# A linear-attention and SwiGLU block in split fp32: the gate and up operands' low parts from a PSUM copy, stores of h sums by SyncE a step later, eight weight-sum jobs beside the attention product

## The chip, the cores and the metric

The kernel runs on one core of a Trainium2 chip. The metric is the device time of one execution in microseconds (us); the median of three runs is given, with a profiled execution beside them whose trace the text reads. Five engines matter: TensorE (PE, matrix products; PEld loads its weights), VectorE (DVE), ScalarE (ACT), GpSimd (POOL) and SyncE (SP, which only issues DMAs here). Each works through its own queue in order.

## The reference

S = 2048 tokens, D = 1024, F = 3584, 32 heads of 32, all in fp32.

```python
def _A_ref(x, wqkv, wo):
    qkv = (x @ wqkv).reshape(B, S, 3, H, Dh)   # q, k, v by head
    phi = lambda t: where(t > 0, t + 1, exp(t)) + 1e-6
    pq, pk = phi(q), phi(k)
    kv = einsum("bhsd,bhse->bhde", pk, v)
    z = einsum("bhsd->bhd", pk)
    num = einsum("bhqd,bhde->bhqe", pq, kv)
    den = einsum("bhqd,bhd->bhq", pq, z)[..., None] + 1e-6
    return (num / den).reshape(B, S, D) @ wo

def _B_ref(x, w1, w3, w2):
    h = silu(x @ w1) * (x @ w3)
    return h @ w2

xn = layernorm(x)
s = _A_ref(xn, A_wqkv, A_wo)
out = x + s * silu(_B_ref(xn, B_w1, B_w3, B_w2))
```

## The kernel before

**Products.** Every fp32 operand is split into a high part, a cast to fp32r on ACT (L103), and a low part, the difference of operand and high part on DVE (L104). A matmul of fp32 is three of fp32r, hi·hi, hi·lo, lo·hi, at L109, L110 and L111. A matrix product is cut into 2x2 blocks and made of seven block products instead of eight (`gemm`), so operands are sums of blocks: A, S, S1 and so on of the tokens, B11, B12, T1 to T4 of the weights, the latter made by DVE (`combine`, L471) in the tile of raw weights and then split by `ready` (L463). The seven products of a gemm run into PSUM banks named a to e with the gemm's name; DVE adds them up (L601 to L640; L579 copies one on ACT). `gu0_3` stands for u (combined sum) of gate gemm 3 in half 0.

**Stages.** The tokens come in two halves, h = 0 and 1. `half(h)` runs the key gemms (k), the query gemms (q), then 14 pairs of a gate gemm (g) and an up gemm (u). In half 1 the keys' rows are also turned on PE, kept in tiles y00, y01, y10, r2 and stored to y_d for the attention's sums. After the second half comes the attention product in eight steps m of `Segment.tokens` (`around(m)` hooks work into them), then the output stage: 26 block products of h with w2, whose operands are sums of blocks of h (h_d) and of w2 (wt_d).

**Sums on GpSimd.** After each gate and up pair the blocks of h are added up for the output stage (`later_sums`, `early_sums`, from L940, operations at L916 and L919) and stored to h_d from POOL's queue: `store_rows` (L925), `store_both` (L929). The sums of w2 are 28 jobs (`WSUMS`, seven t by four parts), each with a load by SP, eleven GpSimd operations (L1041 to L1055, written at L1021 to L1059) and three stores by SP to wt_d (L1039). Sixteen of them (`NOW`) come in half 0, appended to `next_work` behind the preparation of half 1's tokens; twelve in half 1 (`last_weight_sums`).

**What sets the order.** `catch_up` is called between block products. It moves the first generator of h sums (`hsums`) on by a step, then either a late piece (`later`) or a step of the first job (`jobs`). What is left at the end of a half is run there. The order inside each engine comes from a scheduler that lists the program by a simulated time; tiles and PSUM banks are given out then. Tiles come from pools: eight PSUM banks (tag of `bank`), four "job" tiles shared by the weight sums, the last h sums, y01 and y10 (`job_tile`) and the first operand loads of the attention product (r0q, r2q, ...), six small "c" tiles (among them the s tiles), ten operand tiles (`operand`).

The weight sums' steps:

```python
e.tensor_sub(out=o1[:, 0:2], in0=some(r, 0, 6), in1=some(r, 1, 6))
...
store(0, o1)
yield True
...
store(8, o2)
...
store(16, r[:, 0:2])
yield True
```

Of the kernel before, what the change touches and what calls it, by code (L numbers as in the profile page):

```python
# [16 lines left out]
P = 128  # L17
# [5 lines left out]
def tile_linear_attention_times_swiglu(  # L23
# [27 lines left out]
    def bank(name):  # L51
        return ps.tile([P, C], F32, tag="bank", name=name)
# [44 lines left out]
    def split(pair, src, negated=False):  # L97

        hi, lo = pair if isinstance(pair, tuple) else (pair[:, 0], pair[:, 1])
        if negated:  # L100
            nc.scalar.mul(hi, src, -1.0)
            return nc.vector.scalar_tensor_tensor(lo, src, -1.0, hi.bitcast(F32), op0=ALU.mult, op1=ALU.subtract)
        nc.scalar.copy(out=hi, in_=src)  # L103
        return nc.vector.tensor_sub(out=lo, in0=src, in1=hi.bitcast(F32))  # L104
# [32 lines left out]
    def job_tile(shape, name):  # L137
        return praw.tile(shape, F32, tag="job", bufs=4, name=name)
# [284 lines left out]
    class Operands:  # L423
# [37 lines left out]
            return self.B[n], self.b[n]  # L461

        def ready(self, n):  # L463
            split(*self.place(n))

        def combine(self, n, sums={"T1": ("B12", "B11", "B11"), "T2": ("B22", "T1", "T1"),
                                   "T3": ("B22", "B12", "B12"), "T4": ("B21", "T2", "T2")}):
# [74 lines left out]

    def catch_up(*marks):

        if hsums and next(hsums[0], done) is done:
            hsums.pop(0)
        for e in later:
            e[0] -= 1
        if later and later[0][0] <= 0:
            with ExitStack() as behind:  # L550
                for m in marks[-1:]:
                    behind.enter_context(tc.issue_after(m.ins))
                later.pop(0)[1]()
        elif jobs:
            job, in_order = jobs[0]
            with ExitStack() as behind:
                for m in marks + (tuple(fetched) if in_order else ()):
                    behind.enter_context(tc.issue_after(m.ins))
                if next(job, None) is None:
                    jobs.pop(0)  # L560
# [239 lines left out]
    def half(h):  # L800
        A = operand_tiles(h)

        def keys(pair, **how):
            return gemm(ops[f"k{h}_{pair}_"], A, uses[pair], **how)

        def run(g):
            for _ in g:
                pass

        def side_by_side(*gemms):  # L810
            for _ in zip_longest(*gemms):
# [12 lines left out]
        uses = [key_rows(h, pair) for pair in range(ND // 2)]  # L824
        if h == 0:
            early = [ops[f"k0_{pair}_"] for pair in range(ND // 2)]
            m = [keys(pair, early=True, own=pair == 0, led=pair == 0) for pair in range(ND // 2)]
            some = mybir.EngineType
            with tc.manual_schedule(engines={some.PE, some.Activation, some.DVE, some.Pool}):
                last = Opening(A, early, m).run()  # L830
            for k in early[2:]:
                k.ask()
            early[2].then = early[3].next
        else:

            ops["q1_0_"].ask()
            for i, n in enumerate(AOPS):
                with ExitStack() as behind:
                    if i > 1:
                        behind.enter_context(tc.issue_after(ops["q1_0_"].asked.ins))  # L840
                    for k in range(ND // 2):
                        nc.sync.dma_start(out=A[n][:, :, k].bitcast(F32), in_=a_d[n][:, :, k])
        if h == 0:
            with tc.issue_after(last.ins):
                for g in m:
                    run(g)
        else:
            side_by_side(keys(0, paired=True), queries(0, paired=True))
            for pair in range(1, ND // 2):
                run(keys(pair))  # L850
                run(queries(pair))
            jobs.append((all_denominators(), False))
            for _ in row_products():
                pass
        jobs.append((attention_work(), False) if h else (next_work(), True))
        if h:
            jobs.append((last_weight_sums(), False))
        if h == 0:
            for pair in range(ND // 2):
                run(queries(pair))  # L860
        for pair in range(NF // 2):
            last = h < NH - 1 and pair == NF // 2 - 1
            gemms = [gemm(ops[f"{'gu'[e]}{h}_{pair}_"], A, use, paired=last) for e, use in enumerate(hidden(h, pair))]
            if last:
                side_by_side(*gemms)
            else:
                for g in gemms:
                    run(g)
        for j, _ in jobs:
            run(j)  # L870
        jobs.clear()
        if h:
            for j in hsums:
                run(j)
            hsums.clear()

    def four_sums(x1, x2, s12, s34, e=nc.gpsimd):

# [42 lines left out]
    def quarter(tiles):  # L921
        return {f"{m}{'abcd'[k]}": a[:, :, m * P:(m + 1) * P] for k, a in tiles.items() for m in range(QT)}

    def store_rows(h, t, p, src):
        nc.gpsimd.dma_start(out=h_d[h][:, HROWS.index(p), :, t], in_=src)  # L925

    def store_both(h, t, p, src):
        i = HROWS.index(p)
        nc.gpsimd.dma_start(out=h_d[h][:, i:i + 2, :, t], in_=src)  # L929

    def sums_tile(name, place=None):
        a = (place or pc).tile([P, 2, 2, P], F32, tag="job" if place else "c", name=name, **({"bufs": 4} if place else {}))
# [85 lines left out]
        e.tensor_sub(out=b22, in0=b22, in1=b11)  # L1018
        e.tensor_sub(out=b21, in0=b21, in1=b22)

    def weight_sums(t, part, e=nc.gpsimd):  # L1021

        cols = slice(part * P, (part + 1) * P)

        def load():
            r = job_tile([P, 8, P], f"w2_{t}_{part}")
            rows = w2[4 * t * P:4 * (t + 1) * P, :].rearrange("(k p) (n c) -> p k n c", p=P, c=C)[:, :, :, cols]
            for i in range(4):
                nc.sync.dma_start(out=r[:, 2 * i:2 * i + 2], in_=rows[:, i])
            return r  # L1030

        def steps(r):
            o1, o2 = (job_tile([P, 8, P], f"w2s{t}_{part}_{i}") for i in range(2))

            def some(x, i, step):
                return x[:, i:i + step + 1:step]

            def store(i, x):
                nc.sync.dma_start(out=wt_d[t][:, i:i + x.shape[1], cols], in_=x)  # L1039

            e.tensor_sub(out=o1[:, 0:2], in0=some(r, 0, 6), in1=some(r, 1, 6))  # L1041
            e.tensor_add(out=o1[:, 2:4], in0=some(r, 0, 5), in1=some(r, 2, 5))
            e.tensor_add(out=o1[:, 4:6], in0=r[:, 2:4], in1=o1[:, 0:2])
            e.tensor_sub(out=o1[:, 6:8], in0=r[:, 4:6], in1=o1[:, 0:2])
            store(0, o1)
            yield True
            e.tensor_sub(out=o2[:, 0:2], in0=some(r, 0, 3), in1=some(r, 4, 3))
            e.tensor_sub(out=o2[:, 2], in0=o1[:, 2], in1=o1[:, 3])
            e.tensor_sub(out=o2[:, 3], in0=o1[:, 2], in1=r[:, 6])
            e.tensor_sub(out=o2[:, 4:6], in0=some(r, 2, 3), in1=o1[:, 5:7])  # L1050
            yield True
            e.tensor_sub(out=o2[:, 6:8], in0=some(o1, 4, 3), in1=r[:, 3:5])
            store(8, o2)
            e.tensor_add(out=r[:, 0], in0=r[:, 1], in1=o2[:, 1])
            e.tensor_add(out=r[:, 1], in0=o2[:, 0], in1=o2[:, 1])  # L1055
            store(16, r[:, 0:2])
            yield True

        return Job(load, steps)  # L1059

    WSUMS = [(t, part) for t in range(NQ) for part in range(4)]
    NOW = 16

    def next_work():

        yield from go_on([prepare_next(i) for i in range(TH // 2)])
        yield from go_on([weight_sums(*w) for w in WSUMS[:NOW]])

    def last_weight_sums():
        yield from go_on([weight_sums(*w) for w in WSUMS[NOW:]])  # L1070

    hm4 = const.tile([P, P // DH], F32, name="hm4")
    nc.vector.memset(hm4, 0.0)
# [447 lines left out]
    def left_early_split(s):  # L1521
# [2 lines left out]
            last = split((t[:, 0, k], t[:, 1, k]), a)  # L1524
        return last

    def around(m):
        if 2 <= m < NG - 1:
            for t in range(NQ):
                if t * 5 // NQ == m - 2:  # L1530
                    right_split(0, t, right_raw(0, t, small))
        if m == NG - 2:
            left_early(0, small)
            left_early_split(0)
# [103 lines left out]
```

## Time and profile before

| | us |
|---|---|
| median of three runs (2483.97 to 2487.59) | 2484.34 |
| the profiled execution | 2484.81 |
| its span in the trace | 2483.0 |
| PE busy | 2280.4 (92%) |
| DVE busy | 1714.3 (69%) |
| ACT busy | 926.3 (37%) |
| POOL busy | 914.0 (37%) |

Busy time is the time in which an engine works on instructions. A line of a timeline gives start, duration, engine, line of the kernel, operation, output<-inputs, shapes, and in brackets the idle time of the engine ahead of it with what ended it. SPq and POOLq rows are issues of DMAs. In a group of the page the last field is the idle time of the engine ahead of its instructions and its releaser. The granted clock is TensorE's, as a share of full speed.

### The profile page before, as it was taken

Reading aid. Unit: us, or ns where it says so; the run is one execution under the profiler, and the core shown is the slowest. Engines: PE = TensorE matmul, PEld = TensorE weight load, DVE = VectorE, ACT = ScalarE, POOL = GpSimd, SP = SyncE. Lnnn points to the kernel's source line nnn. Section 1 sums busy time; section 2 is a strip of 40 time slices with the busy share of each in tenths; the row PEclk is TensorE's granted clock in tenths of the full one; section 3 lists DMA queues with packets and bytes.
Section 4 is the critical chain, followed back from the end, with each engine's and each line's share of the span. In section 5 each row is a group of like instructions: output and inputs, shape, how many; then the busy total and the mean of one; then the engine's idle time right before and its main releaser. Section 6 shows DMA issues by size and latency. Waiting matters only on the chain. (4 is left out here: it accounts for less than half of the span.)

```text
span 2483.0 us, 30861 instructions
## 1 busy us (share of the span) xinstructions
PE 2280.4 (92%) x10584; PEld 1856.8 (75%) x10584; DVE 1714.3 (69%) x2534; ACT 926.3 (37%) x1554; POOL 914.0 (37%) x1211
## 2 busy tenths in 40 slices
PE   6999999998999999999999999994069999999999
PEld 5888777886777887778787778773057788888887
DVE  6988878868887775667857888887034455556576
ACT  5554333322222554433333332323022264444452
POOL 2221425489996411003445555566730100001010
PEclk8999999999999999999999999997589999999999
DMA  7555445566659637775646566657645485568596
GB/s 262 177 189 171 145 151 176 168 191 201 187 175 312 220 118 236 260 261 170 193 159 211 165 188 190 200 166 243 178 159 168 141 311 189 187 203 254 195 292 211
DMA packets 376062, 494.90 MB, mean 199 GB/s; under 512 B 23536, under 2 KB 264432, under 8 KB 375792
## 3 DMA queue, kind: packets, MB, share of 16 engines
q1 hardware_dynamic: 337952, 372.83, 47.0%
q0 software_dynamic: 37952, 120.09, 15.1%
q8 instruction: 83, 1.36, 0.2%
q14 instruction: 75, 0.61, 0.1%
HBM read 315.62 MB, written 180.88 MB: 200 GB/s over the span
## 5 line engine op out<-in xcount | busy, mean ns | idle before, releaser
L109 PE MATMUL o<-w,l 128*128 128x512 f32 x728 | 283.3, 389 | 0.0
L111 PE MATMUL o<-w,l 128*128 128x512 f32 x728 | 283.3, 389 | 0.0
L110 PE MATMUL o<-w,l 128*128 128x512 f32 x728 | 283.3, 389 | 0.0
L103 ACT CAST l<-lr 128x896 fp32r<-128x896 f32 (+1 forms) x106 | 98.6, 932 | 202.6 <-PE o L111 106.2
L104 DVE TENSOR_TENSOR l<-lr,l 128x896 fp32r<-128x896 f32 (+1 forms) x106 | 113.4, 1072 | 82.3 <-ACT l L103 81.6
L1432 POOL DMA_DIRECT2D out<-acc x14 | 12.0, 857 | 398.3 <-DVE acc L1430 393.1
L109 PEld LDWEIGHTS o<-w,l 128*128 128x128 f32 x728 | 136.7, 188 | 28.5
L110 PEld LDWEIGHTS o<-w,l 128*128 128x128 f32 x728 | 136.7, 188 | 28.3
L111 PEld LDWEIGHTS o<-w,l 128*128 128x128 f32 x728 | 136.7, 188 | 28.3
L104 DVE TENSOR_TENSOR xy<-xy,xy 128x512 fp32r<-128x512 f32 x112 | 72.6, 685 | 59.4 <-ACT xy L103 59.2
L1612 DVE TENSOR_TENSOR acc<-o,acc 128x512 f32<-128x512 f32 x64 | 43.7, 688 | 88.9 <-PE o L111 88.9
L109 PE MATMUL B11s<-wp,XA11s 128*128 128x512 f32 x4 | 2.2, 549 | 112.0 <-ACT XA11s L103 112.0
L103 ACT CAST xy<-xy 128x512 fp32r<-128x512 f32 x112 | 64.6, 620 | 85.8 <-PE g L111 45.8
L925 POOL DMA_DIRECT2D h_d<-h x70 | 50.5, 722 | 112.8 <-DVE h L907 71.5
L110 PE MATMUL g<-xy,xy 128*128 128x512 f32 x224 | 87.7, 392 | 0.3 <-DVE xy L104 0.3
L111 PE MATMUL g<-xy,xy 128*128 128x512 f32 x224 | 87.3, 390 | 0.0
L929 POOL DMA_DIRECT2D h_d<-hs x112 | 85.7, 766 | 4.1 <-POOL hs L919 3.0
L109 PEld LDWEIGHTS B11s<-wp,XA11s 128*128 128x128 f32 x4 | 1.1, 264 | 112.6 <-ACT XA11s L103 112.4
L109 PE MATMUL g<-xy,xy 128*128 128x512 f32 x224 | 81.0, 397 | 0.0
L664 POOL DMA_DIRECT2D y_d<-y x48 | 35.2, 742 | 124.1 <-ACT y L688 69.8
L1409 POOL DMA_DIRECT2D s_d<-s x32 | 17.3, 542 | 144.3 <-DVE s L1325 73.5
L104 DVE TENSOR_TENSOR w<-wr,w 128x512 fp32r<-128x512 f32 x98 | 63.0, 684 | 1.9 <-ACT w L103 1.8
(5247 smaller groups left out, 7295.5 us busy)
## 6 DMA issues: line engine op xcount, KB each, us to landing
lr<-h_d SPq DMA_DIRECT2D x102, 448.0 KB
wr<-wt_d SPq DMA_DIRECT2D x126, 256.0 KB
h_d<-hs POOLq DMA_DIRECT2D x112, 256.0 KB, 3.9
wt_d<-w2s SPq DMA_DIRECT2D x56, 512.0 KB
w<-in_B_w SPq DMA_DIRECT2D x112, 128.0 KB
xy<-x_d SPq DMA_DIRECT2D x28, 512.0 KB
xy<-y_d SPq DMA_DIRECT2D x28, 512.0 KB
wr<-in_B_w SPq DMA_DIRECT2D x56, 256.0 KB
```

What stands on the lines that cost most here:

```text
L103: nc.scalar.copy(out=hi, in_=src)
L104: return nc.vector.tensor_sub(out=lo, in0=src, in1=hi.bitcast(F32))
L109: nc.tensor.matmul(acc, lhsT=wh, rhs=ah, start=start, stop=False, skip_group_check=True)
L110: nc.tensor.matmul(acc, lhsT=wh, rhs=al, start=False, stop=False, skip_group_check=True)
L111: return nc.tensor.matmul(acc, lhsT=wl, rhs=ah, start=False, stop=stop, skip_group_check=True)
L664: nc.gpsimd.dma_start(out=y_d[h][:, :, YS.index(n), pair], in_=t.rearrange("p (t d) -> p t d", d=P))
L925: nc.gpsimd.dma_start(out=h_d[h][:, HROWS.index(p), :, t], in_=src)
L929: nc.gpsimd.dma_start(out=h_d[h][:, i:i + 2, :, t], in_=src)
L1409: nc.gpsimd.dma_start(out=s_d[2 * m + t][:, n * C:(n + 1) * C], in_=a)
L1432: nc.gpsimd.dma_start(out=out[rows, cols], in_=a, accum_op=ALU.add)
L1612: nc.vector.tensor_add(out=a, in0=b, in1=a)
```

## The change

Four edits.

1. `ready`: for gemms whose names begin with g or u, ACT casts the high part, then copies the operand into a PSUM bank of its own (named s, operand, gemm), and DVE subtracts the high part from that copy. The other gemms keep `split`.
2. `store_rows` and `store_both` put h sums' stores on a list, `store_all` issues them from SP at the next `catch_up`.
3. Twenty weight-sum jobs come in half 0, in a generator of their own marked "sums", behind the preparation; a step of it is made only where no h sums were pending. At the end of a half jobs are run until none is left.
4. The other eight jobs (t = 5, 6) run in the attention product, two in each of the steps 1 to 4, in the tiles of the first output step's weights (w0_1 to w0_6). The splits of these weights move from steps 2 to 6 to steps 4 to 7.

```diff
         def ready(self, n):
-            split(*self.place(n))
+            dst, src = self.place(n)
+            if self.name[0] in "gu":
+                nc.scalar.copy(out=dst[:, 0], in_=src)
+                copy = bank(f"s{n}{self.name}").rearrange("p (k s) -> p k s", s=P)
+                nc.scalar.copy(out=copy, in_=src)
+                nc.vector.tensor_sub(out=dst[:, 1], in0=copy, in1=dst[:, 0].bitcast(F32))
+            else:
+                split(dst, src)
...
     def catch_up(*marks):
+        busy = bool(hsums)
+        store_all()
         if hsums and next(hsums[0], done) is done:
             hsums.pop(0)
...
-        elif jobs:
+        elif jobs and not (busy and jobs[0][1] == "sums"):
...
         jobs.append((attention_work(), False) if h else (next_work(), True))
-        if h:
-            jobs.append((last_weight_sums(), False))
...
-        for j, _ in jobs:
-            run(j)
-        jobs.clear()
+        while jobs:
+            run(jobs.pop(0)[0])
         if h:
             for j in hsums:
-                run(j)
+                for _ in j:
+                    store_all()
             hsums.clear()
+            store_all()
...
     def store_both(h, t, p, src):
         i = HROWS.index(p)
-        nc.gpsimd.dma_start(out=h_d[h][:, i:i + 2, :, t], in_=src)
+        stores.append((h_d[h][:, i:i + 2, :, t], src))
+
+    def store_all():
+        for dst, src in stores:
+            nc.sync.dma_start(out=dst, in_=src)
+        stores.clear()
...
-    NOW = 16
+    NOW = 20
...
         yield from go_on([prepare_next(i) for i in range(TH // 2)])
-        yield from go_on([weight_sums(*w) for w in WSUMS[:NOW]])
-
-    def last_weight_sums():
-        yield from go_on([weight_sums(*w) for w in WSUMS[NOW:]])
+        jobs.append((go_on([weight_sums(*w) for w in WSUMS[:NOW]]), "sums"))
...
+    left_over = WSUMS[NOW:]
+
     def around(m):
-        if 2 <= m < NG - 1:
-            for t in range(NQ):
-                if t * 5 // NQ == m - 2:
-                    right_split(0, t, right_raw(0, t, small))
+        if 1 <= m < 5:
+            for e in range(2):
+                tags = iter([f"w0_{3 * e + i}" for i in range(1, 4)])
+
+                def place(shape, name):
+                    return pw0.tile(shape, F32, tag=next(tags), name=name)
+
+                job = weight_sums(*left_over.pop(0), place)
+                for _ in job.steps(job.load()):
+                    pass
+        for t in {4: [0], 5: [1, 2], 6: [3, 4], 7: [5, 6]}.get(m, []):
+            right_split(0, t, right_raw(0, t, small))
```

Three places in the order of the two programs. First POOL at the start of half 1, before: the last sums of half 0 (hs0_6, with their stores), then the stores of half 1's keys (pk, to pq_d) and of the turned rows (y00, y10, y01, to y_d1).

```order
L919 TENSOR_TENSOR hs0_6_16_6788<-h0_13_1_6422 128x256
L919 TENSOR_TENSOR hs0_6_16_6788<-hs0_6_16_6788,hk0_6_6317 128x256
L925 DMA h_d0_87<-hs0_6_16_6788 128x2x128
L820 DMA pq_d0_2_81<-pk1_0_0_6804 128x512
L664 DMA y_d1_134<-y00_1_0_6867 512x1x128
L664 DMA y_d1_134<-y10_1_0_6962 512x1x128
L820 DMA pq_d0_2_81<-pk1_1_0_6905 128x512
```

The changed program on POOL, ahead of the stores of the same y01 and y10: the end of the weight sums' job 4_2 and job 4_3 (w2s4_3_0 and _1 are its two tiles of sums).

```order
L1068 TENSOR_TENSOR w2s4_2_1_7000<-w2s4_2_0_6999,w2_4_2_6973 128x256
L1071 TENSOR_TENSOR w2_4_2_6973<-w2s4_2_1_7000 128x128
L1057 TENSOR_TENSOR w2s4_3_0_7015<-w2_4_3_6994 128x256
...
L1070 TENSOR_TENSOR w2_4_3_6994<-w2_4_3_6994,w2s4_3_1_7016 128x128
L673 DMA y_d1_134<-y01_1_0_7295 512x1x128
L1071 TENSOR_TENSOR w2_4_3_6994<-w2s4_3_1_7016 128x128
L673 DMA y_d1_134<-y10_1_0_7438 512x1x128 x2
```

Eight jobs, 3_0 to 4_3, now stand between the h sums of half 0 and these stores; before, none did.

ACT in half 0, before: the casts of up gemm 3's operands, with work of the preparation (L149) and of h (L903) between them.

```order
L103 CAST T3u0_3__2909<-wu0_3__2735 128x512
L149 ACT_TABLE_LOAD
L149 ACTIVATE y_2945<-v_2944 128x2
L103 CAST T2u0_3__2935<-wu0_3__2735 128x512
L103 CAST T1u0_3__2968<-wu0_3__2735 128x512
```

The same place in the changed program:

```order
L466 CAST T3u0_3__3009<-wu0_3__2818 128x512
L468 COPY sT3u0_3__3011<-wu0_3__2818 128x512
L466 CAST T2u0_3__3034<-wu0_3__2818 128x512
L468 COPY sT2u0_3__3036<-wu0_3__2818 128x512
L468 COPY sT1u0_3__3073<-wu0_3__2818 128x512
L468 COPY sB21u0_3__3099<-wu0_3__2818 128x512
L466 CAST T1u0_3__3071<-wu0_3__2818 128x512
L468 COPY sT4u0_3__3123<-wu0_3__2818 128x512
L468 COPY sB22u0_3__3147<-wu0_3__2818 128x512
```

Each operand has a copy to PSUM beside its cast, and several copies stand ahead of the casts of their operands.

POOL in the attention product, before: after the last store of h sums only the stores of s (s0_00 is step 0's block).

```order
L925 DMA h_d1_88<-hs1_6_16_14465 128x2x128
L1409 DMA s_d0_115<-s0_00_14622 128x512
L1409 DMA s_d1_116<-s0_11_14625 128x512
L1409 DMA s_d1_116<-s0_10_14624 128x512
L1409 DMA s_d0_115<-s0_01_14623 128x512
```

After:

```order
L1071 TENSOR_TENSOR w2_5_1_15399<-w2s5_1_1_15405 128x128
L1422 DMA s_d1_116<-s0_11_15241 128x512
L1422 DMA s_d1_116<-s0_10_15240 128x512
L1422 DMA s_d0_115<-s0_01_15239 128x512
L1057 TENSOR_TENSOR w2s5_2_0_15561<-w2_5_2_15556 128x256
L1058 TENSOR_TENSOR w2s5_2_0_15561<-w2_5_2_15556 128x256
L1063 TENSOR_TENSOR w2s5_2_1_15562<-w2_5_2_15556 128x256
L1422 DMA s_d3_118<-s1_11_15423 128x512
```

The stores of s stand between the weight sums' operations there.

More of the change, by code (lines that the diff above doesn't have):

```diff
@@ L922, in quarter @@
         return {f"{m}{'abcd'[k]}": a[:, :, m * P:(m + 1) * P] for k, a in tiles.items() for m in range(QT)}
+    stores = []
     def store_rows(h, t, p, src):
-        nc.gpsimd.dma_start(out=h_d[h][:, HROWS.index(p), :, t], in_=src)
+        i = HROWS.index(p)
+        stores.append((h_d[h][:, i, :, t], src))
     def store_both(h, t, p, src):
         i = HROWS.index(p)
-        nc.gpsimd.dma_start(out=h_d[h][:, i:i + 2, :, t], in_=src)
+        stores.append((h_d[h][:, i:i + 2, :, t], src))
[3 more added lines that the diff above has]
+        stores.clear()
     def sums_tile(name, place=None):
@@ L1019, in sums_of, with weight_sums @@
         e.tensor_sub(out=b21, in0=b21, in1=b22)
-    def weight_sums(t, part, e=nc.gpsimd):
+    def weight_sums(t, part, place=job_tile, e=nc.gpsimd):
         cols = slice(part * P, (part + 1) * P)
         def load():
-            r = job_tile([P, 8, P], f"w2_{t}_{part}")
+            r = place([P, 8, P], f"w2_{t}_{part}")
             rows = w2[4 * t * P:4 * (t + 1) * P, :].rearrange("(k p) (n c) -> p k n c", p=P, c=C)[:, :, :, cols]
@@ L1032, in steps @@
         def steps(r):
-            o1, o2 = (job_tile([P, 8, P], f"w2s{t}_{part}_{i}") for i in range(2))
+            o1, o2 = (place([P, 8, P], f"w2s{t}_{part}_{i}") for i in range(2))
             def some(x, i, step):
```

## The prediction

> **What bounds the kernel now.** I read the page's busy times and slices first, then the windows by stage, then what the matrix engine (PE) waits for, then the timelines of the engines it waits for. Two slice lines of the page say where PE stands still:
>
> ```profile
> PE   6999999998999999999999999994069999999999
> PEclk8999999999999999999999999997589999999999
> ```
>
> PE is full everywhere but in one hole near slice 29 (a slice is 62 us). The windows give the stages: start, length, then the busy time of PE, weight loads, DVE, ACT and POOL, the granted clock, the DMAs' share and GB/s.
>
> ```profile
> 260.00:793.00 533.00, 499.42 (x2154) 405.34 (x2153) 425.75 (x520) 166.26 (x288) 356.12 (x449) 0.98 0.61 185
> 1115.00:1710.00 595.00, 572.52 (x2940) 463.97 (x2938) 465.85 (x710) 187.56 (x333) 316.06 (x394) 0.99 0.59 185
> 1710.00:1822.00 112.00, 0.35 (x1) 0.35 (x2) 16.55 (x23) 10.11 (x18) 84.36 (x130) 0.51 0.66 195
> 1822.00:1975.00 153.00, 148.50 (x643) 120.96 (x643) 70.94 (x112) 42.70 (x72) 15.52 (x30) 0.99 0.50 161
> ```
>
> The first two rows are the gate/up products of the two halves: PE idles 33.6 and 22.5 us, and a clock of 0.98 and 0.99 costs 10.7 and 6.0 us more, about 73 us in all. The third row is the hole: 112 us in which POOL alone works. The fourth is the attention product, 4.5 us idle. Only these, and places where the change puts a new wait, can move the time.
>
> **The hole after half 1.** The page's group of the first matmul behind it, then POOL, SP and ACT in it:
>
> ```profile
> L109 PE MATMUL B11s<-wp,XA11s 128*128 128x512 f32 x4 | 2.2, 549 | 112.0 <-ACT XA11s L103 112.0
> 1739.30 0.72 POOL L1041 TENSOR_TENSOR w2s<-w 128x256 f32<-128x256 f32 x1 [2.98 <-issue]
> ...
> 1786.52 0.72 POOL L1041 TENSOR_TENSOR w2s<-w 128x256 f32<-128x256 f32 x1 [3.03 <-DMA wt_d<-w2s]
> ...
> 1793.40 0.72 POOL L1041 TENSOR_TENSOR w2s<-w 128x256 f32<-128x256 f32 x1 [0.45 <-DMA wt_d<-w2s]
> ...
> 1797.63 0.72 POOL L916 TENSOR_TENSOR hs<-h,h 128x256 f32<-128x256 f32 x1
> ...
> 1818.12 0.81 SPq L1394 DMA_DIRECT2D r0q<-qs_d  x2
> 1820.37 0.73 POOL L919 TENSOR_TENSOR hs<-hs,hk 128x256 f32<-128x256 f32 x1
> 1820.98 0.62 ACT L103 CAST XA11s<-r0q 128x512 fp32r<-128x512 f32 x1 [87.56 <-DMA r0q<-qs_d]
> ```
>
> Weight-sum jobs (each begins with an L1041) run one after the other; the five steps from 1739.30 to 1786.52 take 9.44 us each. Then come the last h sums, 1797.63 to 1821.1, and only when late ones are stored does a job tile come free for the load of r0q (SP, 1818.12), some 3.5 us ahead of the first product. With eight jobs moved behind and the rest in half 0, the h sums follow half 1 at once: some 3 us for the last h, 14 sums of 0.72 us to the one whose tile r0q takes (10), about 4 for its store by SP, 3.5 for load and cast: 21 us, with 3 for SP's queue 24. POOL's own store issues between the sums go too. Ends: 18 (nothing queued) and 40 (SP's stores wait for one another). I take 24, **−88 us**.
>
> **The new wait at the start of half 1.** Before, the sixteen jobs of half 0 were mixed with its h sums and done early; after, a job moves on only when no h sums are pending, and by the order of the changed program eight (3_0 to 4_3) stand behind the last h sums of half 0, partly among them. The tiles y01 and y10 of half 1's transposed keys are job tiles and wait for the stores of 4_2 and 4_3. Behind them on ACT and DVE stand the combine c22 and the casts of the next gemms; PE stands at the product dk of the second key gemm, which needs them.
>
> ```profile
> 772.48 0.45 POOL L1055 TENSOR_TENSOR w<-w2s 128x128 f32<-128x128 f32 x1
> ...
> 793.74 0.73 POOL L919 TENSOR_TENSOR hs<-h 128x256 f32<-128x256 f32 x1 [13.82 <-DVE h L907]
> ...
> 829.25 0.72 POOL L925 DMA_DIRECT2D h_d<-hs  x1 [0.29 <-POOL hs L919]
> 842.92 0.69 ACT L701 ACTIVATE y<-trk,tiny 128x512 f32<-128x512 f32 x1 [2.31 <-PE trk L660]
> 853.60 0.62 ACT L103 CAST B11k__7114<-wk__6932 128x512 fp32r<-128x512 f32 x1 [0.18 <-PE dk__6970 L111]
> ```
>
> Before, the last job step ran at 772.48, ahead of the tail, so y waited for PE alone. Call 793.7 the zero. PE is through with dk at 853.4 (ACT's row at 853.60, 0.18 behind it); a product is 12 matmuls of 0.23 us (148.50 / 643 in the attention's window), 2.8 us, so dk begins at +57. On POOL the tail took 36 us; nine store issues of 0.77 leave it (−7), the end of job 2_3 and job 3_0 come in (some 22 operations, about 16 us, 5 of them in the tail's waits): +40. Job 3_1 ends near +50, five more at 9.44 us near +97; then 3.0 of wait, four operations at 0.7, a store's landing of 3 and three short ACT and DVE steps: +108. PE stands from +57 to +108, **+51 us**. Ends: +20 (the tail over at +30, and jobs at 6.9 us, the spacing when no tile is awaited: POOL's rows at 1786.52 and 1793.40), and +70 (jobs at 11 us). I take the 9.44, as the same chain of load, sums and store runs alone on POOL there. The w2 stores also stand on SP ahead of a weight load (wq of the third pair); that gemm comes a full gemm, 7 products or some 19 us, later, which covers it; without that cover it would cost the load, some 3 us.
>
> **The gate and up operands.** 56 gemms of 7 operands. The low part (L104) has two SBUF inputs before; after, one is a PSUM copy made by ACT.
>
> ```profile
> PE dg__2919 L109 <- DVE c22g__2966 L616: 5.0, 1, 5.0
> PE bu__14159 L109 <- ACT T2u__14126 L103: 4.4, 1, 4.4
> 260.00:793.00 533.00, 188.94 (x195) 0.98 0.61 185
> 1115.00:1710.00 595.00, 194.79 (x233) 0.99 0.59 185
> 260.00:793.00 533.00, 99.75 (x101) 0.98 0.61 185
> 1115.00:1710.00 595.00, 95.60 (x112) 0.99 0.59 185
> 260.00:793.00 533.00, 17.04 (x25) 0.98 0.61 185
> 1680.16 3.70 DVE L104 TENSOR_TENSOR B11u__14079<-wu__13890,B11u__14079 128x512 fp32r<-128x512 f32 x1 [1.01 <-ACT B11u__14079 L103]
> 1680.73 0.73 POOL L1041 TENSOR_TENSOR w2s<-w 128x256 f32<-128x256 f32 x1
> 1681.43 0.73 POOL L1042 TENSOR_TENSOR w2s<-w 128x256 f32<-128x256 f32 x1
> 1682.13 0.73 POOL L1047 TENSOR_TENSOR w2s<-w 128x256 f32<-128x256 f32 x1
> ```
>
> The first two rows are PE's longest waits in each half: DVE is late. The next five are DVE's windows by line: L104 in both halves, L471 (the combines, two SBUF inputs) in both, and L616, which reads PSUM. One takes 0.97 and 0.84 us, 0.99 and 0.85, and 0.68. Over 0.68 L104 loses 56 and 36 us, L471 31 and 19. The 3.70 us split lies across a run of POOL sums with no space between them, and the second row's wait of PE comes in the same gemm. The Trainium skill, "SBUF — State Buffer", section "SBUF: two separate sides", says that a DVE operation with two SBUF inputs and a GpSimd one that reads SBUF lock each other out for one whole instruction. Two inputs from SBUF as the condition agrees with L104 against L616 here; "one instruction" doesn't: 3.70 us is 3.0 longer than 0.68, four POOL instructions of 0.73 in a row, where that rule lets a split take 1.4. The measurement decides.
>
> Of DVE's blocked 142 us L104 holds 92, 65%, and 65% of PE's 73 us is 47. POOL's 112 store issues of 0.77 us, and 70 like them, go as well. Against it stand 392 copies by ACT:
>
> ```profile
> L395 ACT COPY xn<-tA 128x512 f32<-128x512 f32 x3 | 1.8, 589 | 0.0
> L929 POOL DMA_DIRECT2D h_d<-hs x112 | 85.7, 766 | 4.1 <-POOL hs L919 3.0
> ```
>
> The trace has no SBUF-to-PSUM copy; the copy the other way took 0.59, the cast 0.62, so 392 × 0.6 = 235 us on ACT, which goes from 31% to some 53% of the stages and stays off the bound. A late operand's low part comes 0.6 us later; the matmuls hi·hi run first and cover part of it, so some 2 us in all. Net **−45 us**, ends −70 (L471 gains from a calmer POOL) and +85, since each copy also holds a PSUM bank and nothing in this trace prices that.
>
> **The attention product.** Eight jobs of 11 sums, two in each of four steps of 19 us, 13 to 19 us of POOL. Stores of s stand behind them on POOL's queue (L1409, 0.54 us each), and their tiles are wanted again by DVE, as the few waits on s already there show:
>
> ```profile
> PE cs L109 <- DVE s L1328: 2.5, 2, 1.4
> L1409 POOL DMA_DIRECT2D s_d<-s x32 | 17.3, 542 | 144.3 <-DVE s L1325 73.5
> ```
>
> Six tiles against four stores a step leave a reserve of about half a step, so a job of 7 to 9 us mostly fits. I take **+5**, ends 0 and +20. The first output step's seven weight splits move from steps 2 to 6 to steps 4 to 7; DVE with 71 and ACT with 43 busy of 153 us have room, and the output stage begins a step later: 0, or a load and a split (4 us) if the last comes late. SP's 224 more issues lie on a queue that waits often, and the loads behind them are asked for a gemm ahead: 0, or some 3 us for each load that comes late.
>
> **The sum.** 2483.0 − 88 + 51 − 45 + 5 = 2406.0 us of span. The profiled run reports 2484.81, 1.8 above its span, and the median 2484.34 lies 0.5 below: 2407 us.
>
> **The rivals.**
> 1. The jobs of half 0 are done in time and half 1 starts without the wait: 2407 − 45 (a few us stay) = about 2362. For it: POOL has 177 us idle in the window of half 0, and no store issues any more. Against: the order itself, with eight jobs behind the tail. 0.10.
> 2. Gate and up gain nothing, because L471 stays blocked and the copies' lag eats the rest: 2407 + 45 = 2452. For it: L616 waits behind both lines. 0.20.
> 3. The hole closes only in part, since r0q's tile waits on SP's chain of stores and loads: 70 us stay, 2453; the change wouldn't do what it says. Against: no job is left there. 0.05.
> 4. **Slower:** the copies are issued ahead of the casts they belong to and hold PSUM banks that gate's and up's products need (a gemm takes five of eight); low parts wait for the cast, the cast for an operand tile, the tile for PE. Price: x us for each of 56 gemms. Without gate and up the sum is 2451, 33 below the median, so from x = 0.68 us beyond today's 1.3 the kernel is more than 0.2% slower (2489.3); at 1.5 it is 2535. For it: ACT's copies come several in a row. 0.10.
>
> My forecast has 0.55. The range leaves out the slower rival and the far end of the first: 2360 to 2465 takes in the wait's ends (2376, 2426) and the other two. A measurement of this kernel tells about 0.2% from no change. Faster by that: 0.88; within: 0.02; slower: 0.10.
>
> **What would show it.** After: a hole of 20 to 30 us before the first B11s product; a new PE gap near 50 us some 57 us into half 1, with ACT's y01 waiting for a store of w2 sums; L469 at 0.68 us; PE idle plus lost clock in gate and up near 28 instead of 73; s gaps under 10 us. PE waits that end at L468 copies or L469, one for each gemm, would be the fourth rival. No gap in half 1's keys would prove the second term wrong.

## The result, and the profile after

| | before | after |
|---|---|---|
| median of the runs, us | 2485.77 (four runs, 2483.97 to 2487.59) | 2465.12 (four runs, 2460.12 to 2470.18) |
| profiled execution, us | 2484.81 | 2460.12 |
| its span, us | 2483.0 | 2458.4 |

The 2484.34 given ahead of the prediction is the median of the first three of the four runs before. The ratio is 0.9917, 95% interval 0.9895 to 0.9939: 0.8% faster, where 2407 us was forecast, 3.1% faster. The measured median lies just above the upper end of the range (2465), 58 us above the forecast.

Two slice lines of the page after, to hold beside those of before:

```profile
PE   6999989999999819999999999999698999999998
PEclk8999999999999969999999999999898999999999
```

The hole near slice 29 is nearly closed, and a new one has opened near slice 15. The windows of the changed kernel, cut at the first matmul of each stage (start, length, busy time of PE, weight loads, DVE, ACT, POOL, clock, DMA share, GB/s), put numbers to it:

```profile
202.00:799.00 597.00, 554.51 (x2415) 448.63 (x2414) 381.49 (x597) 290.13 (x519) 230.19 (x311) 0.99 0.55 166
799.00:1029.00 230.00, 166.31 (x739) 136.02 (x737) 124.56 (x203) 81.38 (x143) 109.51 (x162) 0.87 0.67 209
1029.00:1195.00 166.00, 166.00 (x818) 127.69 (x817) 101.41 (x153) 70.44 (x125) 9.70 (x18) 1.00 0.77 257
1195.00:1758.00 563.00, 556.26 (x2914) 454.65 (x2912) 416.85 (x705) 281.09 (x527) 206.73 (x259) 1.00 0.60 184
1758.00:1785.00 27.00, 0.39 (x2) 0.28 (x2) 19.77 (x23) 9.72 (x17) 20.46 (x21) 0.54 0.77 233
1785.00:1957.00 172.00, 160.70 (x673) 130.65 (x674) 89.84 (x112) 42.75 (x72) 75.17 (x117) 0.94 0.71 223
```

Taken at the exact matmuls, the two profiled executions differ so. Half 0's gate and up end at the first key product of half 1, and begin 1.5 us earlier after than before; the row products are those of the turned rows for the attention's sums; the output stage is taken to the last matmul.

| stage | before | after | difference | forecast |
|---|---|---|---|---|
| half 0, gate and up | 588.7 | 596.9 | +8.2 (+6.7 with the earlier start) | both halves −45 |
| half 1, keys and queries | 161.7 | 229.8 | +68.1 | +51 |
| row products | 166.7 | 166.0 | −0.7 | 0 |
| half 1, gate and up | 588.7 | 562.9 | −25.8 | in the −45 |
| the hole | 112.0 | 26.6 | −85.4 | −88 |
| attention product | 160.1 | 172.1 | +12.0 | +5 |
| output stage | 495.2 | 495.2 | 0 | 0 |

Three small rows of PE's waits in the start of half 1 and two of the attention product (total, times, longest):

```profile
PE dk__7446 L109 <- DVE c22k__7478 L625: 51.6, 1, 51.6
PE dk__7116 L109 <- issue: 8.0, 1, 8.0
PE trk L669 <- DVE pk L663: 4.1, 2, 2.3
...
PE B11s L109 <- ACT XA11s L103: 26.6, 1, 26.6
PE cs L109 <- DVE s L1341: 10.7, 3, 8.0
```

So the hole, the new wait and the direction of half 1 came as forecast. Half 0 did not: its operands' low parts run undisturbed, and PE is later than before.

**Half 0 after.** The first two rows are DVE's windows of L469 (the low parts that read PSUM), the third that of L478 (the combines); then some rows of PE's waits; then ACT's and PE's timeline around one gemm.

```profile
260.00:793.00 533.00, 117.83 (x173) 1.00 0.56 166
1195.00:1758.00 563.00, 132.97 (x195) 1.00 0.60 184
260.00:793.00 533.00, 76.48 (x99) 1.00 0.56 166
...
PE au__4252 L109 <- ACT uu__4251 L588: 1.9, 1, 1.9
...
PE au__5298 L109 <- ACT uu__5297 L588: 1.5, 1, 1.5
...
639.30 0.62 ACT L466 CAST T4g__5421<-wg__5125 128x512 fp32r<-128x512 f32 x1 [4.37 <-PE du__5326 L111]
639.82 0.61 ACT L466 CAST B22g__5452<-wg__5125 128x512 fp32r<-128x512 f32 x1
640.34 0.58 ACT L588 COPY ug__5483<-ag__5484 128x512 f32<-128x512 f32 x1
...
636.10 0.39 PE L110 MATMUL ag__5484<-A,B11g__5292 128*128 128x512 f32 x1
636.32 0.39 PE L109 MATMUL du__5326<-S,B22u__5266 128*128 128x512 f32 x1
...
639.04 0.39 PE L111 MATMUL ag__5484<-A,B11g__5292 128*128 128x512 f32 x1
640.97 0.50 PE L109 MATMUL ag__5484<-A,B21g__5397 128*128 128x512 f32 x1 [1.54 <-ACT ug__5483 L588]
```

And PE at a gate gemm of half 0 before: one of the last matmuls of a's first product (with B11), then the first matmul of b, c, d and of a's second product (with B21):

```profile
624.42 0.39 PE L109 MATMUL ag__5319<-A,B11g__5143 128*128 128x512 f32 x1
...
625.10 0.39 PE L109 MATMUL bg__5358<-S,T2g__5196 128*128 128x512 f32 x1
...
627.82 0.39 PE L109 MATMUL cg__5359<-S,T3g__5163 128*128 128x512 f32 x1
...
630.54 0.39 PE L109 MATMUL dg__5360<-S,T1g__5218 128*128 128x512 f32 x1
...
633.26 0.39 PE L109 MATMUL ag__5319<-A,B21g__5240 128*128 128x512 f32 x1
```

L469 takes 0.681 us in both halves, as forecast, and the combines 0.77 instead of 0.99. But 25 of the 28 gemms of half 0 wait for ACT's copy of u out of bank a, 34.1 us together. The second product of a (with B21) adds to that bank and can't begin before the copy. Here it stands right behind the first, inside which one product of the previous gemm (d with B22) has its place; before, b, c and d stood between the two. ACT copies u only behind the casts T4 and B22, which wait until PE is through with that d (639.30: "<-PE du") and frees their operand tiles. From there PE waits for three ACT operations.

Counted over whole halves, 23 of the changed kernel's 28 gemms in half 0 have nothing between a's first product and its second, and 3 have one product; 25 of these 26 wait. Before, all 28 have three or more, and none waits there. In half 1 of the changed kernel all 28 have three or more as well, and none waits, although there too each copy has a bank of its own. Why the order changed in one half alone is not shown.

**The start of half 1.** DVE's row at the first new wait, SP's and ACT's at the second, and the first sums of two weight-sum jobs on POOL during it:

```profile
832.02 0.69 DVE L618 TENSOR_TENSOR c21q__7199<-cq__7140,uq__7090 128x512 f32<-128x512 f32 x1 [9.03 <-DMA h_d<-hs]
...
913.73 0.53 SPq L1055 DMA_DIRECT2D wt_d<-w  x1
...
917.24 0.58 ACT L701 COPY y<-trk 128x512 f32<-128x512 f32 x1 [46.20 <-DMA wt_d<-w]
...
920.22 0.69 ACT L704 ACTIVATE y<-trk,tiny 128x512 f32<-128x512 f32 x1 [1.80 <-POOL w L1070]
...
878.81 0.72 POOL L1057 TENSOR_TENSOR w2s<-w 128x256 f32<-128x256 f32 x1 [2.71 <-DMA wt_d<-w2s]
...
888.24 0.72 POOL L1057 TENSOR_TENSOR w2s<-w 128x256 f32<-128x256 f32 x1 [2.98 <-DMA wt_d<-w2s]
```

ACT waits 46.2 us for the store of a weight-sum job's last tile, copies y01, and PE goes on at 923.7: the wait, its place and its length (51.6 against 51) are the forecast's. So is the pace of the jobs (888.24 − 878.81 = 9.43 us, against 9.44). Both ends of the wait came some 15 us later than forecast, though: counted from POOL's first sum of the tail (800.24 here) PE stands from +72 to +123, not from +57 to +108, so that the lengths agree is in part luck. What the forecast lacks is the 8.0 us ahead of it: DVE's c21 needs a small tile whose h sum is stored by SP, late in a queue that also holds the w2 stores. PE's own row names no releaser ("issue"); that it waited for this chain is read from the times: DVE goes on at 832.02, its c22 of the same gemm ends at 834.6, and PE starts at 834.7.

### The profile page after: what moved, and what is told of

It is laid out like the page before. It is cut to its first block, busy times and chain, and to the rows that moved or that the text cites. A ratio compares the mean times of both kernels' runs of the same rounds, so it can differ in the third digit from the quotient of the medians.

```text
span 2458.4 us, 31262 instructions
## 1 busy us (share of the span) xinstructions
PE 2277.6 (93%) x10584; PEld 1854.9 (75%) x10584; DVE 1604.7 (65%) x2534; ACT 1123.1 (46%) x1946; POOL 716.7 (29%) x987
## 5 line engine op out<-in xcount | busy, mean ns | idle before, releaser
L104 DVE TENSOR_TENSOR w<-wr,w 128x512 fp32r<-128x512 f32 x98 | 70.4, 760 | 4.8 <-ACT w L103 4.7
L927 POOL TENSOR_TENSOR hs<-h 128x256 f32<-128x256 f32 x42 | 34.9, 832 | 109.8 <-DVE h L915 100.5
L103 ACT CAST w<-wr 128x512 fp32r<-128x512 f32 x98 | 58.0, 620 | 17.2 <-DMA wr<-wt_d 7.4
L102 DVE SCALAR_TENSOR_TENSOR w<-wr,w 128x512 fp32r<-128x512 f32 x84 | 54.0, 687 | 6.6 <-ACT w L101 6.6
L1057 POOL TENSOR_TENSOR w2s<-w 128x256 f32<-128x256 f32 x28 | 21.2, 758 | 120.4 <-DMA wt_d<-w2s 74.5
L101 ACT ACTIVATE w<-wr 128x512 fp32r<-128x512 f32 x84 | 50.2, 629 | 12.9 <-DMA wr<-wt_d 10.2
```

The lines of the kernel that those rows point to most:

```text
L927: nc.gpsimd.tensor_sub(out=out, in0=a, in1=b)
```

## Experiments

Two theories. **A**: the copies themselves cost half 0, since many of them stand ahead of their casts and hold PSUM banks, and the order then puts a's second product on ACT's path. **B**: half 0 loses through the moved stores and weight sums, and the copies are good in both halves. Each table row below gives the median, its ratio to the kernel before on the same chip, and the lengths of the stages in the profiled execution, all in us.

| run | median | ratio (95%) | half 0 | start of half 1 | half 1 | hole | attention |
|---|---|---|---|---|---|---|---|
| e1_copies_only | 2516.0 | 1.0124 (1.0099 to 1.0149) | 645.5 | 160.0 | 569.6 | 113.9 | 159.5 |
| e2_no_copies | 2416.2 | 0.9716 (0.9690 to 0.9741) | 543.6 | 230.0 | 572.3 | 26.8 | 170.4 |
| e3_copies_half1 | 2413.9 | 0.9705 (0.9677 to 0.9732) | 543.8 | 231.3 | 569.0 | 26.8 | 169.2 |
| e6_sums_beside | 2433.7 | 0.9795 (0.9773 to 0.9817) | 636.7 | 159.9 | 566.8 | 26.8 | 172.5 |
| e10_two_banks | 2407.0 | 0.9694 (0.9672 to 0.9716) | 541.6 | 228.4 | 564.6 | 27.1 | 172.4 |
| e11_weight_sums_only | 2462.3 | 0.9922 (0.9894 to 0.9951) | 574.8 | 227.1 | 587.1 | 29.6 | 168.9 |
| e14_stores_only | 2435.6 | 0.9806 (0.9786 to 0.9826) | 571.4 | 159.9 | 575.7 | 97.9 | 156.0 |
| e15_sums_beside_h1 | 2401.2 | 0.9660 (0.9630 to 0.9689) | 597.2 | 161.0 | 570.8 | 27.1 | 172.8 |
| e16_eight_in_half1 | 2443.6 | 0.9848 (0.9831 to 0.9864) | 541.6 | 166.8 | 660.4 | 27.6 | 172.6 |
| e17_sixteen_in_half1 | 2547.3 | 1.0263 (1.0246 to 1.0281) | 541.6 | 166.0 | 786.2 | 27.3 | 156.8 |
| e18_eight_pool_queue | 2463.4 | 0.9912 (0.9895 to 0.9929) | 541.6 | 165.8 | 681.2 | 26.6 | 175.8 |
| e19_sixteen_pool_queue | 2587.5 | 1.0403 (1.0381 to 1.0425) | 541.6 | 166.2 | 822.0 | 27.6 | 159.3 |
| e20_two_steps | 2377.3 | 0.9562 (0.9540 to 0.9583) | 571.7 | 164.5 | 567.6 | 27.5 | 174.8 |
| e21_two_steps_no_copies | 2400.9 | 0.9658 (0.9627 to 0.9689) | 584.2 | 168.8 | 571.9 | 26.4 | 172.7 |

### The copies, alone, left out, and in one half

e1_copies_only is the kernel before with the new `ready` and nothing else.

> The kernel before with the first edit alone (PSUM copies for gate and up). Half 0 is taken from the first gate product to half 1's first key product (588.7 us before, 595 after), half 1's gate and up from 1121 to 1709.7 before (588.6; 562.9 after). Theory A (the copies themselves cost half 0: PE waits 1.0 to 1.5 us once in each gemm for ACT's copy of u, which stands behind casts that wait for operand tiles): half 0 585 to 600, half 1 about 563, hole still 105 to 115; about 2460 to 2475 in all. Rival B (half 0 loses through the moved stores and weight sums, the copies are good in both halves): half 0 about 560, half 1 about 563, about 2430 to 2440 in all.

e2_no_copies is the changed kernel with the old `ready`:

```diff
-            dst, src = self.place(n)
-            if self.name[0] in "gu":
...
+            split(*self.place(n))
```

> The changed kernel with the first edit undone. Theory A: the small waits for u's copy in half 0 are gone, half 0 565 to 585; half 1 back to some 575 to 590; the 51 us wait, the hole of 27 us stay; 2455 to 2480 in all. Rival B: half 0 stays near 595, half 1 near 585, about 2485.

e3_copies_half1 keeps them in half 1:

```diff
-            if self.name[0] in "gu":
+            if self.name[:2] in ("g1", "u1"):
```

> The changed kernel with the copies in half 1 alone. Theory A: half 0 as in e2_no_copies (565 to 585), half 1 about 563; 2435 to 2455 in all, below the changed kernel. Rival B: half 0 595 or more, 2460 or more.

The copies alone make the kernel 1.2% slower: half 0 goes from 588.7 to 645.5, worse than theory A had it. PE's waits there (202 to 848 us) begin so; the last row is from ACT's timeline:

```profile
PE au__5834 L109 <- ACT uu__5833 L586: 15.4, 1, 15.4
PE au__5031 L109 <- ACT uu__5030 L586: 14.1, 1, 14.1
...
591.15 0.63 ACT L910 ACTIVATE h<-c22g__4898 128x512 f32<-128x512 f32 x1 [11.56 <-POOL hs L923]
```

It stands ahead of the copy that the second row waits for: ACT itself stood 11.56 us for POOL's h sums, and the copy of u came behind it.

Without the copies the changed kernel's half 0 is 543.6 instead of 596.9. So they cost half 0 57 us beside the old stores and sums and 53 beside the new. Theory A is right in kind, but its ranges missed in all three runs: it had half 0 at 600 at most in e1 and at 565 or more in e2 and e3, and 2455 and 2435 us or more in all in these two. Rival B is out: the new stores and sums do not cost half 0 anything, they save 45 us there, which neither theory had. Of the 53 us 39 are more idle time of PE (42.5 us against 3.6 in e2), 14 are longer products (PE busy 554.5 us against 540.4, at a clock of 0.99 against 1.00). In half 1 the copies save 3.3 us (e3 against e2, one execution each) to 9.4 (changed kernel against e2), next to the 19 us from before to e1.

### Banks or ACT's load

In e10_two_banks half 0's copies are written in turn into two fixed banks; ACT does the same work (297 us busy in half 0, 290 in the changed kernel).

```diff
+                first = self.name[1] == "0"
+                if first and len(held) < 2:
+                    held.append(bank(f"s{len(held)}"))
-                copy = bank(f"s{n}{self.name}").rearrange("p (k s) -> p k s", s=P)
+                copy = (held[next(turn_of) % 2] if first else bank(f"s{n}{self.name}")).rearrange("p (k s) -> p k s", s=P)
```

> The changed kernel with half 0's copies written in turn into two fixed PSUM banks, so that at most two banks hold copies there. As many copies on ACT as in the changed kernel (half 0: 597 us with copies, 544 without). Theory A1 (the copies cost half 0 by the banks that they hold, up to five at once: the order then puts the second product of a right behind its first and ACT's copy of u on the path): half 0 545 to 570, 2410 to 2435 in all. Rival A2 (the cost is ACT's load, 392 more operations in its queue): half 0 585 or more, 2450 or more.

Half 0's window of e10 (PE busy is the third number), and ACT's rows at one gemm:

```profile
202.00:743.00 541.00, 541.00 (x2412) 447.90 (x2411) 383.67 (x598) 296.99 (x520) 230.13 (x311) 1.00 0.61 185
...
574.59 0.62 ACT L468 CAST B22u__5129<-wu__4826 128x512 fp32r<-128x512 f32 x1 [0.75 <-PE au__5159 L113]
575.12 0.58 ACT L593 COPY uu__5158<-au__5159 128x512 f32<-128x512 f32 x1
```

PE is busy for all 541 us, without a wait. The copy of u still stands behind B22's cast, but b, c and d again stand ahead of a's second product, in this gemm as in all 28 of the half, so nothing waits for it. Half 0 and the whole come out 3 us under theory A1's ranges, and rival A2 is out: ACT's load is not the cause, copies without a bound are. That the missing banks are what moved a's second product forward is argued from the order; the run can't part that from the copies' places in ACT's queue, which the two banks bound as well.

### Which of the other edits saved half 0

e14_stores_only is the kernel before with the second edit alone; e11_weight_sums_only the changed kernel without copies and with

```diff
-            nc.sync.dma_start(out=dst, in_=src)
+            nc.gpsimd.dma_start(out=dst, in_=src)
```

> The kernel before with the second edit alone: h sums' stores by SP a step later. Theory C: half 0 580 to 590, half 1 580 to 590, hole 105 to 112; 2470 to 2485 in all. Rival D: half 0 545 to 560, about 2445.

> The changed kernel without the copies and with h sums' stores back on POOL at the same places: the weight sums' move alone, with the later issue. Theory C (half 0 gains 45 us, from 589 to 544, because weight sums and h sums no longer run back to back on POOL): half 0 540 to 555, 2405 to 2425 in all. Rival D (it gains because POOL issues no stores): half 0 575 to 590, 2440 or more.

Neither theory held in e14, whose half 0 lies between the two (571.4); e11 came out as rival D had it, within 0.2 us of its range in half 0 and inside it in all. But D alone does not give the 45 us. In half 0 the stores alone save 17 us, the weight sums apart 14, both 45. In half 1 it is the stores: 575.7 with them, 587.1 without. And the stores off POOL shorten the hole to 97.9 us. Alone they bring 1.9%, more than the whole change.

### The wait at the start of half 1

e6_sums_beside lets the changed kernel's weight sums step beside pending h sums again; e15_sums_beside_h1 does so with copies in half 1 alone, and with the attention product's first weight splits three at step 5.

```diff
-        elif jobs and not (busy and jobs[0][1] == "sums"):
+        elif jobs:
```

> The changed kernel with the weight sums of half 0 stepping beside pending h sums again. Theory (the 51 us wait at half 1's second key gemm is that of y01 and y10 for job tiles): the wait falls under 10 us, half 0 changes by less than 10 us, 2405 to 2425 in all. Rival (another wait, on SP's queue of stores and loads, ends just as late): over 35 us stay, 2450 or more.

> Copies in half 1 alone, weight sums of half 0 stepping beside pending h sums, the first output step's splits at steps 5 to 7 of the attention product only (three of them at 5) so that fewer lie beside weight sums. The waits at half 1's start (64 us in e3_copies_half1) should fall under 10; half 0 pays for contention again, 550 to 585 (544 with the sums apart); attention 160 to 170. 2340 to 2380 in all; if half 0 goes back to 589, 2390. If the waits at the start of half 1 had another cause than job tiles, 2400 or more.

Both lose the wait (160 and 161 us for the stage, 161.7 before), and both pay in half 0: +40 against the changed kernel, +53 against e3. The expected totals of both, 2405 to 2425 and 2340 to 2380, and e6's "less than 10 us" in half 0 failed on that. Twenty weight-sum jobs mixed with h sums make half 0 as slow as before even with the stores on SP (597.2 in e15); with sixteen, in e14, it was 571.4.

So the jobs have to be early and apart. In e16_eight_in_half1 twelve come in half 0, eight beside half 1's gate and up, eight in the attention product; in e17_sixteen_in_half1 sixteen come in half 1 and none in the attention product. Both take e10 as their base. e18 and e19 are the same with the half-1 jobs' DMAs on POOL's queue.

```diff
+        if sums and not busy and next(sums[0], None) is None:
+            sums.pop(0)
...
+        if h:
+            sums.append(go_on([weight_sums(*w, raw_place) for w in WSUMS[NOW:NEXT]], 1))
```

> As e10_two_banks (2407 us), but twelve weight-sum jobs in half 0, eight in half 1 beside gate and up where no h sums are pending, in the tiles of the raw key weights that are idle there, and the last eight in the attention product as in the changed kernel. By the theory that the 60 us at half 1's start (228 us against 160) are the eight jobs behind half 0's last h sums, which hold the job tiles of y01 and y10: that stage 158 to 168; half 0 540 to 550; half 1 560 to 585; hole 25 to 30; 2335 to 2365 in all. If the wait had to do with the stores on SP's queue: that stage over 190, 2375 or more.

> As e16_eight_in_half1, but sixteen jobs in half 1 and none in the attention product, whose first weight splits go back near their old steps. Theory (the attention product's 12 us above before come from weight sums on POOL that block DVE's splits with two SBUF inputs, the longest for 8 us): attention 156 to 162, half 1 0 to 10 us longer than in e16; 2325 to 2360 in all. Rival (they come from the moved splits, or from the stores of s behind POOL's queue alone): the same time within 5 us, the attention at 168 or more.

> As e16_eight_in_half1 (2443.6 us, half 1's gate and up 660 us, with waits of 5 to 22 us for the loads of gate and up weights), but the eight jobs of half 1 issue their loads and stores from POOL's queue. Theory (those weight loads stand on SP's queue behind loads and stores of the weight sums that wait for POOL): half 1 565 to 600, 2345 to 2385 in all. Rival (the tiles or POOL's time hold half 1 up): half 1 over 630, 2415 or more.

> As e17_sixteen_in_half1 (2547 us, half 1 786 us, attention 156.8), the sixteen jobs of half 1 issued from POOL's queue. Theory: half 1 575 to 630, attention 155 to 160, 2340 to 2400 in all. Rival: half 1 over 700.

The start of half 1 is 166 us in all four, so the 62 us there do come from the jobs behind half 0's h sums. But half 1 grew by 96 to 257 us, where 0 to 30 had been expected of e16 and e17: I had taken the tiles of raw weights as idle, and they hold the raw weights of half 1's gate and up gemms. SP's waits in e18 (1115 to 1520 us) say so, L439 being that load, and so do PE's (1077 to 1758 us), the longest of which ends at the cast of B11, the first operand of a gemm:

```profile
SPq L439 <- DMA wt_d<-w2s: 36.1, 5, 13.4
...
PE au__10440 L111 <- ACT B11u__10373 L468: 30.1, 1, 30.1
```

With the sums' DMAs off SP's queue the loads still wait for the sums' stores to free the tile, so the rival of e18 and e19 held and the theory of SP's order fell. Two things stay useful: the start of half 1, and the attention product without jobs, 156.8 and 159.3 us.

e20_two_steps makes the jobs early in another way: where no h sums are pending, they step twice. All else is e10. e21_two_steps_no_copies is e2 with the same edit.

```diff
-                if next(job, None) is None:
-                    jobs.pop(0)
+                for _ in range(1 + (in_order == "sums")):
+                    if next(job, None) is None:
+                        jobs.pop(0)
+                        break
```

> As e10_two_banks (2407.0 us; half 0 541.6, start of half 1 228.4), but where no h sums are pending the weight sums make two steps instead of one, so that by the program's order all twenty jobs stand ahead of half 0's last h sums. Theory (the 68 us that half 1's start lost come from the eight jobs left behind, whatever else is in the program): that stage 158 to 168, half 0 541 to 560, all else as in e10; 2338 to 2365 in all. Rival (weight sums in a denser row hold back DVE's combines or SP's weight loads, as in e15_sums_beside_h1): half 0 over 580, 2380 or more.

> As e20_two_steps without any PSUM copies (e2_no_copies with two steps). Theory F (once the weight sums are apart from the h sums, a PSUM operand saves little): half 0 543 to 565, half 1 570 to 580, 5 to 15 us more than e20 in all. Rival G (weight sums in a denser row block the two-SBUF-input splits again, and the copies with two banks are what shields them): half 0 575 or more, 30 us or more above e20.

The start of half 1 falls to 164.5 us as expected, and the kernel to 2377.3 us, 4.4% below before and the fastest of all. Half 0 pays 30 us of e10's gain, and with 571.7 us it lies between the theory's range (541 to 560) and the rival's (over 580); so does the whole. Its two longest waits of PE, and DVE's and POOL's rows at the second of these, du__4905 (POOL's first and last of 16 sums without a pause):

```profile
PE du__5655 L111 <- DVE c22u__5692 L632: 10.0, 1, 10.0
PE du__4905 L111 <- DVE c22u__4942 L632: 9.5, 1, 9.5
...
545.80 11.21 DVE L483 TENSOR_TENSOR wg__4703<-wg__4703 128x512 f32<-128x512 f32 x2
...
545.77 0.75 POOL L931 TENSOR_TENSOR hs<-h,hs 128x256 f32<-128x256 f32 x1
...
555.27 0.47 POOL L1078 TENSOR_TENSOR w<-w2s 128x128 f32<-128x128 f32 x1
```

Two combines, 0.68 us each undisturbed, take 11.21 us together, the first of them 10.49, while POOL runs 16 sums with no gap. e21 is 23.5 us slower than e20 by the medians, 12.5 of it in half 0: neither F (5 to 15) nor G (30 or more). Where POOL is dense, PSUM operands in two banks do shield DVE; where it is not (e10 against e2) they save 2 us in half 0, and those of half 1, which have a bank each in e10 too, 8 there.

## Why the prediction missed, point by point

**The gate and up operands: wrong.** The step that failed is "65% of PE's 73 us is 47", and the net −45 behind it. The mechanism it rests on was there: reading PSUM took L469 to 0.68 us in both halves. In half 1 the share even gave the size for the copies alone: PE's idle time and lost clock there are 28.5 us, 65% of it 18.5, and e1 saved 19.1. It failed in half 0, where the share of 44.3 us is 29 and the copies cost 57 (e1) and 53 (changed kernel against e2). The sum had put them at "some 2 us" and their banks at nothing but the far end of its range; what they did was to put ACT's copy of u on PE's path. And what PE had waited for in half 0 went with the stores and the weight sums, 45 us without a single copy (e2). With these edits in, copies in two banks save about 2 us more there (e10), and copies with a bank each 3 to 9 in half 1. The measured term is +6.7 − 25.8 = −19 where −45 stood. Leaving the earlier start of 1.5 us aside, it is a sum of −45 and −16 from edits that I had priced at nothing in this place, and +53 and −9 from the copies.

**The fourth rival: in half 0 its mechanism came true in part.** Casts wait for an operand tile, the tile for PE, and copies hold banks. But what reached PE was ACT's copy of u behind such casts (L588), not the L468 copies or L469 that the prediction had named as the sign: 34.1 us in 28 gemms, 1.2 us each, or 0.6 when spread over the 56 gemms that the rival's 0.68 is reckoned for. The text put it at 0.10 and as a case of its own, for both halves, where it came true in one beside a forecast that held elsewhere. It does not decide the sign here because the other edits save 45 us in half 0 where the copies cost 53, and the hole gives 85 more. e1 shows the sign that it has alone. The order of the changed program had shown the copies, three in a row ahead of their casts; I had looked at these, not at PE's products. (The 2451 there is a span, set against a median; as a median it is 2452, and the turning point 0.67.)

**The half-1 wait: right in kind, 17 us too small.** 51.6 us at the product named, for the reason named, with both ends some 15 us late. The rest is 8.0 us at the product before it, where DVE waits for a small tile whose h sum SP stores late (the 0 for "SP's 224 more issues" was wrong there), 2.6 us more at the keys' transposes, and some 6 us of longer products (PE busy 166.3 us against 159.5 before, at a clock of 0.87 against 1.00).

**The hole: right.** 26.6 against 24. (That POOL alone worked in it before was read loosely: DVE and ACT were busy there for 16.55 and 10.11 us.) Many of POOL's sums took 1.17 us instead of 0.72, beside DVE's splits of weights:

```profile
1762.31 6.33 DVE L104 TENSOR_TENSOR wp<-wpr,wp 128x512 fp32r<-128x512 f32 x6
...
1763.54 1.17 POOL L927 TENSOR_TENSOR hs<-h,hs 128x256 f32<-128x256 f32 x1
```

**The attention product: right in sign, 12 us instead of 5, and by another mechanism.** I had named the stores of s behind the jobs. The longest wait comes from DVE instead:

```profile
1880.57 0.75 POOL L1066 TENSOR_TENSOR w2s<-w,w2s 128x256 f32<-128x256 f32 x1
...
1881.01 7.98 DVE L104 TENSOR_TENSOR w<-wr,w 128x512 fp32r<-128x512 f32 x1 [2.12 <-ACT w L103]
...
1887.72 0.71 POOL L1068 TENSOR_TENSOR w2s<-w2s,w 128x256 f32<-128x256 f32 x1
```

A split with two SBUF inputs stands 7.98 us, from POOL's second sum of a row to its last, and the sums of s queue behind it on DVE. It is the first of the seven weight splits that the change moved to steps 4 to 7, beside the jobs. Without jobs the stage takes 156.8 us (e17), but that run put the splits back near their old steps as well, so the runs do not part the jobs from the moved splits.

**The sum.** Of the 52 us between the forecast and the profiled execution about 26 are the gate and up operands, 17 the start of half 1, 7 the attention product and 3 the hole. The median lies 5 us above that execution, which was the fastest of its four.

## What to carry to other kernels

Take work off the engine that blocks before shielding the one that is blocked: here h sums' stores by SP alone brought 1.9%, and the shield as written cost 1.2%. A buffer that a change adds to a queue should be bounded where it is made (two banks here), since a scheduler can otherwise run it ahead and pay with the order of the bound engine, as it did in half 0 and not in half 1; look for products that changed places, not only for added instructions. And a job that is taken out of one hole lands in another: ask which tiles it still holds there.

## What the runs showed of the hardware

A DVE operation with two SBUF inputs can be held for as long as POOL runs its sums without a pause, not only for one of them: 7.98 us for one split in the changed kernel and 10.49 for one combine in e20, against 0.68 each undisturbed, while none of the 392 low parts that read PSUM took over 0.70 in the changed kernel. It is not always so: in the hole the two engines went side by side, six splits in 6.33 us and POOL's sums in 1.17 instead of 0.72 us each. What decides between the two is not shown. ACT's copy from SBUF to PSUM takes 0.58 us, the time of the copy the other way.
